# A gated mix of a spectral transform and an MLP, with gradients: the MLP as five passes over all rows, in memory of its own beside the transform

## The chip, the cores and the metric

The kernel runs on one core of a Trainium2 chip. A core has TensorE (PE, matrix products into PSUM), VectorE (DVE), ScalarE (ACT), GpSimd (POOL) and SyncE (SP, here only a queue that issues DMAs), each with its own instruction queue worked off in order, and DMA engines that move data between HBM and the on-chip memory SBUF. The metric is the device time of one execution in microseconds (us); of several runs the median counts.

## The reference

Inputs are bf16. S is 2048 rows, D is 1024, F is 3584. What has to come out is the mixed output and the gradients of eight inputs (not of B_x, which is a constant that the forward pass does not use).

```python
def A(x, w_r, w_i):                       # spectral branch
    X = rfft2(x.astype(float32)) * (w_r + 1j * w_i)
    return irfft2(X, s=(S, D)).astype(bfloat16)
def B(x, w1, b1, w2, b2):                 # MLP branch
    h = x @ w1 + b1
    r = where(h > 0, h, 0)
    return (r * r) @ w2 + b2
g   = sigmoid((A_x * gate_w).sum(-1, keepdims=True))
out = g * A(A_x, A_w_r, A_w_i) + (1 - g) * B(A_x, B_w1, B_b1, B_w2, B_b2)
# returned: out, then d(out . grad_out) by A_x, w_r, w_i, w1, b1, w2, b2, gate_w
```

The MLP is six products of the same size: h (x by w1), dh (the gradient by w2 turned, times 2 r), out (h squared by w2), dx (dh by w1 turned), dW2 (h squared turned by the gradient) and dW1 (x turned by dh). Each is 896 matmuls of 128x512.

## The kernel before

The program is written with a tile framework. The kernel names tiles in pools, the framework orders the instructions of each engine before the run, puts in the waits, and pulls an instruction forward when its inputs and tiles are free by the framework's own reckoning; on the chip each engine then follows that order. A pool that is opened where another was closed gets its memory only when the closed pool is done.

All of the work stands in one function. Rows are taken as 16 tiles of 128 (row p*16+t is partition p of tile t). DMAs go alternately through SP and POOL by `dma` (L170, the issuing line of most DMAs is L171); some name SP themselves. Its stages:

- **Rows** (L289 to L304): for each of 16 tiles the input row x and the gradient row go through `load_row` (L280: load, eight turns of 128x128 on PE, a copy by ACT into xT or goT) and `s1` (L247: adds on VectorE, eight matmuls into pk, a copy ft by ACT, eight column matmuls into pu, L266, a copy u, a store to z_scr). The gate of each row is computed here (sgate, gcol; omg is one minus the gate).
- **Middle** (L382 to L418): eight pairs of frequencies; `spectrum` (L313), the products with the weights w, `inverse` (L350), a store to y_scr; the gradients of w_r and w_i. The weights come by the loads of L385.
- **Transform out** (L424 to L460): 32 rows; r is read back from y_scr (L427), matmuls pki (L431) and pui (L437), ACT copies rt and e, adds, a store to a_scr or gx_scr.
- **Scaling** (L462 to L472): the turned gradient goT is multiplied by omg.
- **Row blocks** (L512 to L655): four times, for 512 rows each: 28 times a block of 128 hidden columns (ph, L550; ReLU and square by ACT, L554, L555; pd, L558; dhT by VectorE, L559; eight turns ptr, L566, to have h and dh with rows on partitions, copies into h2S and dhS, L568, L570, stores to h2_scr and dh_scr); then out (acc, L586) with w2 chunks w2c loaded anew for each block of rows and each half of the columns; then dx (accg, L643) with turned w1 chunks, made in the first row block (L618) and read back as w1Ttc in the other three.
- **Weight gradients** (L659 to L734): x and gradient rows lie in SBUF as 2 x 16 tiles, h and dh come by groups of 512 hidden columns (`load_fg`, L669), dW2 (L695) and dW1 (L703), then row sums for the gradients of b2 and gate_w as 64 matmuls (L713, L719), and that of b1.

The transform's pools (fconst, fbuf, fps2, fps1) are closed at the end of the transform; those of the MLP (p1blk, p1w, p1s, p1ps, p1acc, p1tr) are opened after that in the same memory, and those of the weight gradients after these.

Of the kernel before, what the change touches and what calls it, by code (L numbers as in the profile page):

```python
# [10 lines left out]
P = 128  # L11
# [6 lines left out]
FDT = FP16  # L18
# [112 lines left out]
def kernel(  # L131
# [30 lines left out]
    S2, DC, DW, DCH, FC = g.S2, g.DC, g.DW, g.DCH, g.FC  # L162
# [5 lines left out]
    dma_rr = _RR([nc.sync, nc.gpsimd])  # L168

    def dma(out, in_):  # L170
        return dma_rr().dma_start(out=out, in_=in_)  # L171
# [6 lines left out]
    pers = ctx.enter_context(tc.tile_pool(name="pers", bufs=1))  # L178
    dram = ctx.enter_context(tc.tile_pool(name="dram", bufs=1, space=bass.MemoryType.DRAM))

    identb = pers.tile([P, P], BF16, name="identb", tag="identb")
    dma(identb[:], cten["identb"].ap())
    pxt_ctx = ExitStack()
    pxt = pxt_ctx.enter_context(tc.tile_pool(name="pxt", bufs=1))
    xT = pxt.tile([P, DC, S], BF16, name="xT", tag="xT")
    goT = pxt.tile([P, DC, S], BF16, name="goT", tag="goT")

    gatew_bc = pers.tile([P, D], BF16, name="gatew_bc", tag="gatew_bc")
    dma(gatew_bc[:], gate_w.partition_broadcast(P))
    gcol = pers.tile([P, S2], FP32, name="gcol", tag="gcol")  # L190
    omg = pers.tile([P, S2], FP32, name="omg", tag="omg")
    gcs = pers.tile([P, S2], FP32, name="gcs", tag="gcs")
    gpg = pers.tile([P, S2], FP32, name="gpg", tag="gpg")
    aGo = pers.tile([P, S2], FP32, name="aGo", tag="aGo")
    bGo = pers.tile([P, S2, DCH], FP32, name="bGo", tag="bGo")
    dsc = pers.tile([P, S2], FP32, name="dsc", tag="dsc")
    dsc_bf = pers.tile([P, S2], BF16, name="dsc_bf", tag="dsc_bf")
    gb1part = pers.tile([P, FC, g.NSB], FP32, name="gb1part", tag="gb1part")
    b1col = pers.tile([P, FC], FP32, name="b1col", tag="b1col")
    ones_bf = pers.tile([P, P], BF16, name="ones_bf", tag="ones_bf")  # L200
    nc.vector.memset(ones_bf[:], 1.0)
    b2row = pers.tile([1, D], BF16, name="b2row", tag="b2row")
    dma(b2row[:], B_b2.rearrange("(o d) -> o d", o=1))

    with tc.tile_pool(name="b1tmp", bufs=1) as tp_, tc.tile_pool(name="b1ps", bufs=1, space=bass.MemoryType.PSUM) as pp_:
        b1row = tp_.tile([FC, P], BF16, name="b1row")
        dma(b1row[:], B_b1.rearrange("(fc p) -> fc p", p=P))
        b1ps = pp_.tile([P, FC], BF16, name="b1ps")
        nc.tensor.transpose(b1ps[:], b1row[:], identb[:FC, :FC])
        nc.vector.tensor_copy(out=b1col[:], in_=b1ps[:])  # L210

    a_scr = dram.tile([S2, P, D], FDT, name="a_scr")
    gx_scr = dram.tile([S2, P, D], FDT, name="gx_scr")
    z_scr = [dram.tile([S2, P, D], FDT, name=f"z_scr{T}") for T in range(2)]
    y_scr = [dram.tile([S2, P, D], FDT, name=f"y_scr{T}") for T in range(2)]
    SC = S // P
    w2T_scr = dram.tile([FC, P, DC, P], BF16, name="w2T_scr")
    w1T_scr = dram.tile([DCH, FC, P, DW], BF16, name="w1T_scr")
    h2_scr = dram.tile([g.FG, SC, P, g.FGW], BF16, name="h2_scr")
    dh_scr = dram.tile([g.FG, SC, P, g.FGW], BF16, name="dh_scr")  # L220

    YS = inv_sd / XS
    sgate = pers.tile([P, S2], FP32, name="sgate", tag="sgate")
    Q = D // 4
    H = 2 * Q
    LW = g.Df + 1
    with ExitStack() as fx:
        fc_ = fx.enter_context(tc.tile_pool(name="fconst", bufs=1))
        fb = fx.enter_context(tc.tile_pool(name="fbuf", bufs=1))
        ps2 = fx.enter_context(tc.tile_pool(name="fps2", bufs=3, space=bass.MemoryType.PSUM))  # L230
        ps1 = fx.enter_context(tc.tile_pool(name="fps1", bufs=2, space=bass.MemoryType.PSUM))

        def const(name, dt=FDT):
            arr = consts[name]
            t_ = fc_.tile(list(arr.shape), dt, name="k_" + name, tag=name)
            nc.sync.dma_start(out=t_[:], in_=cten[name].ap())
            return t_

        kf = const("kf")
        cf = const("cf")  # L240
        amat = const("amat")
        sgn = const("sgn", FP32)
        ki = const("ki")
        ci = const("ci")
        apmat = const("apmat")

        def s1(T, i, xt, kmat):  # L247
            uv = fb.tile([P, 2, H], FDT, name="uv", tag="uv", bufs=2)
            nc.vector.tensor_tensor(out=uv[:, 0, :], in0=xt[:, 0:H], in1=xt[:, H:D], op=ALU.add)
            nc.vector.tensor_tensor(out=uv[:, 1, :], in0=xt[:, 0:H], in1=xt[:, H:D], op=ALU.subtract)  # L250
            f = fb.tile([P, 4, Q], FDT, name="f", tag="f", bufs=2)
            a0, a1 = uv[:, :, 1:Q], uv[:, :, H - 1 : Q : -1]
            nc.vector.tensor_tensor(out=f[:, 0:2, 1:Q], in0=a0, in1=a1, op=ALU.add)
            nc.vector.tensor_tensor(out=f[:, 2:4, 1:Q], in0=a0, in1=a1, op=ALU.subtract)
            nc.gpsimd.tensor_copy(out=f[:, 0::3, 0:1], in_=uv[:, :, 0:1])
            nc.gpsimd.tensor_copy(out=f[:, 2:0:-1, 0:1], in_=uv[:, :, Q : Q + 1])
            pk = ps2.tile([P, 8, P], FP32, name="pk", tag="ps2")
            fl = f[:].rearrange("p a b -> p (a b)")
            for b in range(8):
                nc.tensor.matmul(pk[:, b, :], lhsT=fl[:, b * P : (b + 1) * P], rhs=kmat, start=True, stop=True)  # L260
            ft = fb.tile([P, 8, P], FDT, name="ft", tag="ft", bufs=2)
            nc.scalar.copy(out=ft[:], in_=pk[:])  # L262
            pu = ps2.tile([P, 2, H], FP32, name="pu", tag="ps2")
            o = 0
            for (b, bank, lo, n, st) in FWD:
                nc.tensor.matmul(  # L266
                    pu[:, bank, lo : lo + n], lhsT=ft[:, b, :], rhs=cf[:, o : o + n],
                    start=bool(st & 1), stop=bool(st & 2), skip_group_check=True,
                )
                o += n  # L270
            u = fb.tile([P, H, 2], FDT, name="u", tag="u", bufs=3)
            nc.any.tensor_copy(out=u[:].rearrange("p j b -> p b j"), in_=pu[:])
            dma(z_scr[T][:].rearrange("c (p i) l -> i (c p) l", i=S2)[i], u[:].rearrange("p j b -> p (j b)"))


        FWD = (
            (4, 0, 0, H, 1), (0, 0, 0, Q + 1, 0), (1, 0, 0, Q + 1, 0), (5, 0, Q + 1, Q - 1, 2),
            (6, 1, 0, Q, 1), (7, 1, 0, Q, 2), (2, 1, Q, Q, 1), (3, 1, Q, Q, 2),
        )
        def load_row(i, T):  # L280
            xt = fb.tile([P, D], BF16, name=f"nat{T}", tag=f"nat{T}", bufs=2)
            dma(xt[:], (go_perm if T else x_perm)[i])
# [23 lines left out]
        def pair(m):  # L306
            return (m, S2 - m) if m else (0, S2 // 2)
# [457 lines left out]
```

## Time and profile before

| what | us |
|---|---|
| runs | 2092.59, 2093.56, 2100.51; median 2093.56 |
| the profiled execution | 2091.43 |
| its span, first to last instruction | 2089.6 |
| PE busy in it | 1642.3 (79%) |
| VectorE busy | 566.9 (27%) |
| ScalarE busy | 564.1 (27%) |
| POOL busy | 447.5 (21%) |

The page of the profile gives these sums, a line of tenths per engine over 40 slices, the DMA queues and the costliest groups of instructions. Other views of the trace used below: busy time by stretches of time, groups by source line, the instructions of one tile, and instructions in order of time. A row of a group has, behind the bar, the busy time and the mean length of one instruction, and behind the second bar how long the engine was idle just before such instructions, with what ended that idle time. Matmuls are pipelined, so the length of one is more than its share of PE's time. A line with "x8" in the timeline is eight instructions merged.

### The profile page before, as it was taken

How to read it: one execution, taken by the hardware profiler on the slowest of the kernel's cores; microseconds unless marked ns; L12 is line 12 of the kernel's file. 1: busy time of each engine (PE TensorE's matmuls, PEld its weight loads, DVE VectorE, ACT ScalarE, POOL GpSimd, SP SyncE). 2: the span in 40 equal slices, each digit the busy share in tenths (PEclk: the TensorE clock that was granted, in tenths of full speed). 3: DMA queues.
4: the chain of work that ended last, by engine and by line, in shares of the span. 5: the costliest groups of instructions: out<-in, count | busy, mean ns of one | idle time of the engine just before them, and what ended most of it. 6: DMA issues, size and time to landing. Idle time of an engine off the chain costs nothing. (4 is left out here: it accounts for less than half of the span.)

```text
span 2089.6 us, 23144 instructions
## 1 busy us (share of the span) xinstructions
PE 1642.3 (79%) x8586; PEld 772.8 (37%) x8586; DVE 566.9 (27%) x1272; ACT 564.1 (27%) x786; POOL 447.5 (21%) x784
## 2 busy tenths in 40 slices
PE   5555555454588887899878998779978789999998
PEld 4442222232244433444323443234423234444443
DVE  4447997432522112222122221122211100000000
ACT  5662323333344312244001430004430011111111
POOL 2220101000422125322122221222131332221200
PEclk8887775555799999999999999999988989999999
DMA  6334433322366556655444554345483463333310
GB/s 211 117 101 146 160 117 118 124 97 86 118 220 204 169 177 194 191 176 186 152 142 153 180 162 161 123 130 181 156 292 106 141 212 119 119 110 101 105 38 28
DMA packets 184401, 304.09 MB, mean 146 GB/s; under 512 B 24207, under 2 KB 120991, under 8 KB 184032
## 3 DMA queue, kind: packets, MB, share of 16 engines
q1 hardware_dynamic: 138480, 161.78, 23.9%
q0 software_dynamic: 45808, 140.83, 20.7%
q8 instruction: 67, 1.10, 0.2%
q14 instruction: 46, 0.38, 0.1%
HBM read 206.03 MB, written 96.49 MB: 145 GB/s over the span
## 5 line engine op out<-in xcount | busy, mean ns | idle before, releaser
L586 PE MATMUL acc<-w2c,h2T 128*128 128x512 bf16 x896 | 216.0, 397 | 47.2 <-DMA w2c<-in_B_w_dram 38.3
L550 PE MATMUL ph<-xT,w1g 128*128 128x512 bf16 x896 | 235.8, 386 | 0.4 <-ACT rT L554 0.4
L643 PE MATMUL accg<-w1Ttc,dhT 128*128 128x512 bf16 x672 | 171.9, 393 | 57.0 <-DMA w1Ttc<-w1T_scr 48.6
L695 PE MATMUL pw<-go,h2l 128*128 128x512 bf16 x896 | 201.5, 387 | 10.6 <-ACT wo L697 4.3
L703 PE MATMUL pw<-dhl,x 128*128 128x512 bf16 x896 | 194.5, 379 | 0.0
L558 PE MATMUL pd<-goT,w2Tfc 128*128 128x512 bf16 x672 | 160.2, 379 | 0.0
L643 PEld LDWEIGHTS <-dhT 128*128 128x128 bf16 x896 | 87.5, 100 | 180.6 <-issue 105.5
L586 PEld LDWEIGHTS <-h2T 128*128 128x128 bf16 x896 | 90.3, 101 | 168.5 <-issue 77.8
L568 ACT COPY h2S<-ptr 128x512 bf16<-128x512 bf16 x112 | 65.7, 586 | 313.4 <-PE ptr L566 217.6
L695 PEld LDWEIGHTS <-h2l 128*128 128x128 bf16 x896 | 88.6, 99 | 122.3 <-issue 13.7
L559 DVE SCALAR_TENSOR_TENSOR dhT<-pd,rT 128x512 bf16<-128x512 f32 x112 | 77.3, 691 | 201.8 <-PE pd L558 194.3
L703 PEld LDWEIGHTS <-x 128*128 128x128 bf16 x896 | 87.5, 98 | 105.9
L715 DVE CAST r<-pb 1x512 bf16<-1x512 f32 x2 | 1.4, 680 | 400.7 <-PE pb L713 400.7
L554 ACT ACTIVATE rT<-ph,b1col 128x512 bf16<-128x512 f32 x112 | 77.1, 689 | 119.3 <-PE ph L550 117.8
L550 PEld LDWEIGHTS <-w1g 128*128 128x128 bf16 x896 | 79.9, 99 | 58.6 <-issue 5.6
L697 ACT CAST wo<-pw 128x512 bf16<-128x512 f32 x56 | 32.9, 587 | 253.1 <-PE pw L695 240.6
L266 PE MATMUL pu<-k_cf,ft 128*128 128x256 f16 (+3 forms) x256 | 48.8, 347 | 59.9 <-ACT ft L262 59.9
L555 ACT ACTIVATE h2T<-rT 128x512 bf16<-128x512 bf16 x112 | 70.4, 629 | 90.2 <-PE acc L586 80.3
L558 PEld LDWEIGHTS <-w2Tfc 128*128 128x128 bf16 x672 | 65.5, 98 | 78.9 <-issue 1.0
L437 PE MATMUL pui<-k_ci,rt 128*128 128x256 f16 (+3 forms) x256 | 63.7, 425 | 37.5 <-ACT rt L433 37.5
L597 DVE SCALAR_TENSOR_TENSOR ot<-a_pc,gcs,bsc 128x512 bf16<-128x512 f16 x32 | 23.8, 750 | 242.6 <-ACT bsc L595 236.5
L171 POOL DMA_DIRECT2D out_dram<-wo x56 | 30.4, 542 | 276.1 <-ACT wo L705 140.8
(209 smaller groups left out, 2109.1 us busy)
## 6 DMA issues: line engine op xcount, KB each, us to landing
w1g<-in_B_w_dram SPq DMA_DIRECT2D x14, 1024.0 KB, 5.4
w1g<-in_B_w_dram POOLq DMA_DIRECT2D x14, 1024.0 KB, 6.3
w2c<-in_B_w_dram SPq DMA_DIRECT2D x28, 512.0 KB, 3.5
w2c<-in_B_w_dram POOLq DMA_DIRECT2D x28, 512.0 KB, 4.0
w2Tfc<-w2T_scr SPq DMA_DIRECT2D x42, 256.0 KB, 3.9
w2Tfc<-w2T_scr POOLq DMA_DIRECT2D x42, 256.0 KB, 3.5
w1Ttc<-w1T_scr SPq DMA_DIRECT2D x84, 128.0 KB, 2.1
w1Ttc<-w1T_scr POOLq DMA_DIRECT2D x84, 128.0 KB, 2.3
```

The lines of the kernel that those rows point to most:

```text
L266: nc.tensor.matmul(pu[:, bank, lo : lo + n], lhsT=ft[:, b, :], rhs=cf[:, o : o + n], start=bool(st & 1), stop=bool(st & 2), skip_group_che ...
L437: nc.tensor.matmul(pu[:, bank, lo : lo + n], lhsT=rt[:, b, :], rhs=ci[:, o : o + n], start=bool(st & 1), stop=bool(st & 2), skip_group_che ...
L550: nc.tensor.matmul(ph[:], lhsT=w1g[:, dc, fcg * P : (fcg + 1) * P], rhs=xT[:, dc, cols], start=(dc == 0), stop=(dc == DC - 1))
L554: nc.scalar.activation(rT[:], ph[:], ACT.Relu, bias=b1col[:, fc : fc + 1])
L555: nc.scalar.activation(h2T[:, fc, :], rT[:], ACT.Square)
L558: nc.tensor.matmul(pd[:], lhsT=w2Tf[:, ec, :], rhs=dbT[:, ec, cols], start=(ec == 0), stop=(ec == DC - 1))
L559: nc.vector.scalar_tensor_tensor(out=dhT[:, fc, :], in0=pd[:], scalar=2.0, in1=rT[:], op0=ALU.mult, op1=ALU.mult, accum_out=gb1part[:, fc, ...
L568: nc.scalar.copy(out=stg[:, :, fcg * P : (fcg + 1) * P], in_=ptr[:])
L586: nc.tensor.matmul(accs[i][:], lhsT=h2T[:, fc, i * P : (i + 1) * P], rhs=w2c[:, r_, :], start=(fc == 0), stop=False)
L643: nc.tensor.matmul(accs[i][:], lhsT=dhT[:, fc, i * P : (i + 1) * P], rhs=w1Tt[:], start=(fc == 0), stop=(fc == FC - 1))
L695: nc.tensor.matmul(pw[:], lhsT=h2l[sc][:, fb * P : (fb + 1) * P], rhs=db_t[sc][:, ecols], start=(sc == 0), stop=(sc == SC - 1))
L703: nc.tensor.matmul(pw[:], lhsT=x_t2[sc][:, db * P : (db + 1) * P], rhs=dhl[sc][:], start=(sc == 0), stop=(sc == SC - 1))
```

## The change

The function is rewritten below the constants. The transform's arithmetic stays, and so does that of the MLP; order, memory and transfers change.

- Loads go through SP (`ld`), stores through POOL (`st`).
- Pools have a side: the transform's SBUF pools (f1, f2, f3) and two PSUM pools (fps, four banks; tps, two banks, for turns of both parts) on the right, the MLP's on the left. Their sizes are such that f2 (the largest of the transform) and the pools of the first MLP pass lie in SBUF together. A pool that takes the place of a closed one waits tile by tile (`reuse_waits="tile"`), not for the whole pool.
- `load_rows` also scales the gradient row by omg and turns the scaled row into dbT, so the stage that scaled goT goes. The transform's matrices for the middle come by pair (two loads for each m), not whole.
- Pass 1 and 2 (`mlp_in`): h and dh for one block of 128 hidden columns over all 2048 rows, xT and dbT resident; w1 and w2 are turned once here; h and dh are stored in both forms.
- Pass 3 and 4 (`mlp_grads`): dW2 with the scaled gradient rows resident, then dW1 with the x rows resident, each over seven groups of 512 hidden columns.
- Pass 5 (`mlp_out`), in two halves: out with all of w2 resident, dx with all of turned w1 resident, by blocks of 256 rows of the turned h and dh.
- The bias b2 is added by VectorE and not by a matmul; the row sums are kept by VectorE and end in two f32 matmuls each.

The new parts in the order in which the program runs them, cut:

```diff
+    ld, st = nc.sync.dma_start, nc.gpsimd.dma_start
+    def pool(name, side="left", space=SBUF, stack=None, bufs=1):
...
+        kw = {} if space == DRAM else dict(side=side, reuse_waits="tile")
...
+    fps, fps_s = pool("fps", "right", PSUM)
+    tps, tps_s = pool("tps", "right", PSUM)
...
+    def load_rows():
+        fb, fbs = pool("f1", "right")
...
+        for i in range(NT):
...
+            turned(xT, xt, i, nc.scalar.copy)
...
+            nc.vector.tensor_scalar(out=db[:], in0=go[:], scalar1=omg[:, c_], scalar2=None, op0=ALU.mult)
+            turned(dbT, db, i, nc.vector.tensor_copy)
...
+            one_s1(fb, cf, 0, i, xt, kf[:])
+            one_s1(fb, cf, 1, i, go, kg[:])
...
+    def mlp_in():
+        wb, wbs = pool("m1")
+        mps, mpss = pool("mps1", "left", PSUM)
...
+        for fp in range(FC // 2):
+            w1g = wb.tile([P, DC, PW], BF16, name="w1g", tag="w1g", bufs=2)
+            ld(out=w1g[:], in_=w1v[:, :, fp * PW : (fp + 1) * PW])
+            h2S = wb.tile([P, NT, PW], BF16, name="h2S", tag="stg", bufs=3)
+            dhS = wb.tile([P, NT, PW], BF16, name="dhS", tag="stg", bufs=3)
+            for f2 in range(2):
...
+                h2T = wb.tile([P, S], BF16, name="h2T", tag="h2T", bufs=2)
+                dhT = wb.tile([P, S], BF16, name="dhT", tag="dhT", bufs=2)
+                for sb in range(S // SW):
...
+                        mm(ph[:], lhsT=w1g[:, dc, fs], rhs=xT[:, dc, ss], start=(dc == 0), stop=(dc == DC - 1))
...
+                        mm(pd[:], lhsT=w2T[:, ec, :], rhs=dbT[:, ec, ss], start=(ec == 0), stop=(ec == DC - 1))
...
+                        st(out=w1T_scr[fc], in_=w1T[:].rearrange("p c d -> p (c d)"))
+                    if sb % 2 == 1:
...
+                            eng = nc.scalar.copy if (k_ == 0 and sb == 1) else nc.vector.tensor_copy
+                            eng(out=stg[:, b0 : b0 + 8, fs], in_=ptr[:])
...
+                st(out=h2T_scr[fc], in_=h2T[:])
+                st(out=dhT_scr[fc], in_=dhT[:])
+            fg, pr = divmod(fp, NPR)
+            st(out=h2_scr[fg][:, :, pr * PW : (pr + 1) * PW], in_=h2S[:])
+            st(out=dh_scr[fg][:, :, pr * PW : (pr + 1) * PW], in_=dhS[:])
...
+    def mlp_grads():
+        wb, wbs = pool("m2")
...
+        def group(scr, fg):
+            t_ = wb.tile([P, NT, FGW], BF16, name="grp", tag="grp", bufs=2)
+            ld(out=t_[:], in_=scr[fg][:])
...
+            ld(out=db[:], in_=go_perm[t])
...
+            nc.vector.tensor_scalar(out=db[:], in0=db[:], scalar1=omg[:, t : t + 1], scalar2=None, op0=ALU.mult)
...
+                V(out=acc[:], in0=acc[:], in1=db[:], op=ALU.add)
...
+    BW = 2 * P
+    def blocks(wb, scr):
+        v_ = scr[:].rearrange("c p s -> p c s")
+        def one(k):
+            t_ = wb.tile([P, FC, BW], BF16, name="hblk", tag="hblk", bufs=2)
+            ld(out=t_[:], in_=v_[:, :, k * BW : (k + 1) * BW])
...
+    def mlp_out():
+        wp, wps = pool("w2p")
+        w2 = wp.tile([P, FC, D], BF16, name="w2", tag="w2")
+        w1T = wp.tile([P, FC, D], BF16, name="w1Tr", tag="w1Tr")
...
+        for fc in range(0, FC, 4):
+            ld(out=w2[:, fc : fc + 4, :], in_=B_w2[fc * P : (fc + 4) * P, :].rearrange("(q p) e -> p q e", p=P))
...
+                    acc = mps.tile([P, H], FP32, name="acc", tag="acc", bufs=4)
+                    for fc in range(FC):
+                        mm(acc[:], lhsT=cur[:, fc, t2 * P : (t2 + 1) * P], rhs=w2[:, fc, cs], start=(fc == 0), stop=(fc == FC - 1))
...
+    run(chain(load_rows(), fft_mid(), fft_out()))
+    run(mlp_in())
+    run(mlp_grads())
+    tps_s.close()
+    fps_s.close()
+    run(mlp_out())
```

`run` only exhausts a generator, so the program names the transform's instructions first, then those of each pass.

More of the change, by code (lines that the diff above doesn't have):

```diff
@@ L188 @@
-    gatew_bc = pers.tile([P, D], BF16, name="gatew_bc", tag="gatew_bc")
[L189 to L210, printed above, removed]
@@ L435 @@
[L435 to L442 removed]
+                pu = fps.tile([P, 2, H], FP32, name="pui", tag="ps2", bufs=2)
+                column_stage(INV, pu, rt, ci)
@@ L738, with chain, run @@
+    def chain(*gens):
+        for g_ in gens:
+            yield from g_
+    def run(gen):
+        for _ in gen:
+            pass
+    run(chain(load_rows(), fft_mid(), fft_out()))
[4 more added lines that the diff above has]
+    run(mlp_out())
 _INS = ['A_x', 'A_w_r', 'A_w_i', 'B_x', 'B_w1', 'B_b1', 'B_w2', 'B_b2', 'gate_w', 'grad_out']
```

833 lines of the change are left out of this document (384 added, 449 removed).

## The prediction

> **What bounds the kernel now.** First the busy time by stretch, cut where the stages change: rows (stage 1 of the transform), middle, transform out, scaling of the turned gradient, four row blocks of the MLP, weight gradients, tail. The columns are busy us of each engine with instructions, granted clock, DMA share, GB/s.
>
> ```profile
> core 0: us, PE busy (x) PEld busy (x) DVE busy (x) ACT busy (x) POOL busy (x), PEclk, DMA share, GB/s
> 0.00:171.00 171.00, 96.21 (x793) 72.65 (x793) 73.81 (x185) 104.88 (x116) 37.20 (x104) 0.82 0.43 148
> 171.00:345.00 174.00, 100.58 (x473) 38.02 (x474) 160.98 (x257) 48.90 (x42) 17.06 (x24) 0.69 0.40 129
> 345.00:541.00 196.00, 91.53 (x491) 54.84 (x489) 70.77 (x195) 61.68 (x64) 11.38 (x21) 0.53 0.32 102
> 541.00:560.00 19.00, 11.76 (x52) 5.63 (x52) 16.96 (x17) 5.42 (x17) 15.47 (x5) 0.60 0.35 117
> 560.00:1668.00 1108.00, 934.22 (x4923) 420.15 (x4921) 239.52 (x615) 277.43 (x436) 276.03 (x462) 0.96 0.53 171
> 1668.00:2070.00 402.00, 394.46 (x1795) 176.39 (x1796) 2.04 (x5) 65.28 (x112) 88.82 (x167) 0.98 0.34 111
> 2070.00:2089.60 19.60, 13.54 (x64) 5.16 (x62) 2.84 (x5) 0.46 (x1) 1.56 (x3) 0.98 0.02 7
> ```
>
> The reader is to see three states. The transform takes 541 us with PE busy 288 at a clock of 0.82 to 0.53; VectorE is full only in the middle (161 of 174). The row blocks are PE's, yet not at its rate. The weight gradients are nearly that rate, which the chain of waits in order of time gives, with the first and last of the pieces that repeat:
>
> ```profile
> 1710.65 27.63 PE pw L703 x128
> ...
> 1904.03 27.63 PE pw L695 x128
> ```
>
> 128 matmuls of 128x512 in 27.63 us are 0.216 us each. The MLP has six products of 896, so 5376 x 0.216 = 1161 us that both kernels need. The four row blocks hold 3584 of them (774 us) and 1344 turns of 128x128; 1108 - 774 - 75 leaves 259 us. The groups by line say what PE waited for:
>
> ```profile
> L586 PE MATMUL acc<-w2c,h2T 128*128 128x512 bf16 x896 | 216.0, 397 | 47.2 <-DMA w2c<-in_B_w_dram 38.3 <-DVE gx L648 4.2 <-DVE bGo L602 4.0
> L643 PE MATMUL accg<-w1Ttc,dhT 128*128 128x512 bf16 x672 | 171.9, 393 | 57.0 <-DMA w1Ttc<-w1T_scr 48.6 <-DVE bGo L602 6.4 <-DVE gx L648 0.9
> L523 PE MATMUL ptw<-identb,w2r 128*128 128x128 bf16 x224 | 18.3, 228 | 25.5 <-ACT h2S L568 20.3 <-DMA w2r<-in_B_w_dram 5.2
> L431 PE MATMUL pki<-k_ki,r 128*128 128x128 f16 x256 | 33.2, 311 | 68.7 <-DMA r<-y_scr 68.6
> L266 PE MATMUL pu<-k_cf,ft 128*128 128x256 f16 (+3 forms) x256 | 48.8, 347 | 59.9 <-ACT ft L262 59.9
> ```
>
> Single durations here are pipelined and no rate; the idle column counts. Weight chunks that arrive just in time (38.3, 48.6), staging copies held by a store (20.3); in the transform, y rows (68.6) and ACT's evictions (59.9). The rest of the 259 lies between matmuls. The waits are latencies with no other work placed behind them.
>
> Is other work put there when there is some? The tile views of w and w2c, and PE's timeline in the first row block:
>
> ```profile
> L385 SPq DMA_DIRECT2D w<-in_A_w_r_dram x8: 373/375/657, 20.7 to 289.0; - x8
> L171 SPq DMA_DIRECT2D w2c<-in_B_w_dram x28: 367/381/529, 568.6 to 1575.0; - x28
> 616.74 0.61 PE L523 MATMUL ptw<-identb,w2r 128*128 128x128 bf16 x8
> 617.19 1.24 PE L550 MATMUL ph<-xT,w1g 128*128 128x512 bf16 x5
> 618.27 1.89 PE L558 MATMUL pd<-goT,w2Tf 128*128 128x512 bf16 x8
> 620.00 0.39 PE L566 MATMUL ptr<-identb,h2T 128*128 128x128 bf16 x4
> 620.22 0.81 PE L550 MATMUL ph<-xT,w1g 128*128 128x512 bf16 x3
> 621.03 0.40 PE L566 MATMUL ptr<-identb,dhT 128*128 128x128 bf16 x4
> 621.26 0.61 PE L523 MATMUL ptw<-identb,w2r 128*128 128x128 bf16 x8
> ```
>
> The transform's w loads stand behind the whole row loop in the program, yet the first goes at 20.7, about 150 us ahead; w2c goes at 568.6, while the blocks of h and dh still have to run (the cycle shown is at 617). And three ph of the next block stand before the last turns (ptr of dhT) of the present one. So the order on an engine is not that of the program: work whose tiles are free is pulled forward. In the kernel before, the MLP's pools take the transform's place, so nothing of it could be.
>
> **The change part by part.** *PE's own work.* One block of 128 hidden columns in this cycle takes 621.26 - 616.74 = 4.52 us for 16 matmuls and 16 turns; 8 turns are 617.19 - 616.74 = 0.45, one 0.056. At the rate it would be 16 x 0.216 + 16 x 0.056 = 4.35, so a factor of 1.04. The first pass does per block of 128, over all 2048 rows, 64 matmuls and 48 turns: 13.8 + 2.7 = 16.5, with the factor 17.2; 28 blocks 481 us. The transform at full rate: rows 32 x (16 turns 0.90 + 2305 columns 0.97) = 60; middle 32 x 8 x 0.216 = 55 and some 216 small ones at a turn's price, 12, together 67; out 32 x (0.45 + 0.97) = 45. Sum 172.
>
> *VectorE and ScalarE in the first pass.* Prices:
>
> ```profile
> L559 DVE SCALAR_TENSOR_TENSOR dhT<-pd,rT 128x512 bf16<-128x512 f32 x112 | 77.3, 691 | 201.8 <-PE pd L558 194.3 <-issue 3.8 <-ACT rT L554 3.2
> L559 DVE DVE_READ_ACCUMULATOR dhT<-pd,rT 128x1 f32 x112 | 9.3, 83 | 0.0
> L346 DVE CAST x<-px 128x1024 f16<-128x1024 f32 x16 | 19.5, 1220 | 20.5 <-PE px L345 20.5
> L300 DVE TENSOR_SCALAR kg<-k_kf,gcol 128x128 f16<-128x128 f16 x16 | 4.0, 252 | 5.7 <-ACT gcol L297 5.7
> L570 DVE COPY dhS<-ptr 128x512 bf16<-128x512 bf16 x112 | 47.6, 425 | 138.5 <-DMA dh_scr<-dhS 74.7 <-PE ptr L566 53.8 <-PE pd L558 10.0
> L445 DVE TENSOR_TENSOR tt<-e 128x512 f16<-128x512 f16 x32 | 13.6, 426 | 115.7 <-ACT e L443 115.7
> L371 DVE TENSOR_TENSOR pc<-v 128x1024 f16<-128x1024 f16 x14 | 9.7, 690 | 1.8 <-ACT v L367 1.6
> L286 ACT COPY goT<-pt 128x1024 bf16<-128x1024 bf16 x16 | 16.3, 1018 | 0.0
> L554 ACT ACTIVATE rT<-ph,b1col 128x512 bf16<-128x512 f32 x112 | 77.1, 689 | 119.3 <-PE ph L550 117.8 <-issue 1.4
> L555 ACT ACTIVATE h2T<-rT 128x512 bf16<-128x512 bf16 x112 | 70.4, 629 | 90.2 <-PE acc L586 80.3 <-POOL goT L472 6.6
> ```
>
> A turned 128x1024 piece in bf16 on VectorE isn't in the trace; it lies between 0.43 (one of 512) and 0.85 (two). I take 0.69, as the two add rows go from 426 at 512 to 690 at 1024. Per block VectorE then has 4 x (0.69 + 0.08 to read the accumulator) + 5 x 0.69 = 6.5 us, 183 in all; ScalarE 4 x (0.69 + 0.63) + 1.02 = 6.3. Both are under PE's 17.2.
>
> *Stage A, transform with the first pass beside it.* They lie in separate SBUF and PSUM, so I expect the pulling forward seen above, transform first.
> Rows: bound by a chain of PE, ACT, PE, ACT per half row; ACT loses the goT copy (16 x 1.02), VectorE gains scale and turn. 171 before; I take 155 (145 to 171). Only two blocks can be open (h2T and dhT have two buffers), so PE does at most 1.8 blocks here.
> Middle: VectorE's 161 of transform work stay and come first. What the MLP gets of it lies between nothing (stage 174, no block) and 70 us (stage 238, 10.7 blocks, PE then full). I take 35, near the low end because the stage is 92% full already: 5.4 blocks in (161 + 35)/0.97 = 202.
> Rest: PE has 45 + (28 - 1.8 - 5.4) x 17.2 = 403, VectorE about half of it, so PE sets it: 403.
> Staging: h2S and dhS share three buffers, so each pair of blocks waits for the store of the pair before. Same bytes as before, where PE lost 20.3 to them and VectorE 74.7; I take 14, between 0 and 75.
> Queues: all loads now stand on SP, some 150 in A at 0.3 to 0.5 us of issue each, and a w1g that waits for its buffer holds the transform's next z or r behind it. Between nothing and the 68.6 that y rows cost PE before; I take nothing, since PE has blocks to do meanwhile. On POOL the small f copies of the row loop stand behind stores that wait for evictions; only two blocks store there, nothing.
> A = 155 + 202 + 403 + 14 = 774. With nothing in the middle the rest is 45 + 26.2 x 17.2 = 496 and A = 155 + 174 + 496 + 14 = 839; with all of it 155 + 238 + 311 + 14 = 718.
> The terms 172 and 45 want a full clock. The transform ran at 0.53 in its last stage (row 345 to 541). At 0.53 the 45 are 85, A is 40 longer. I take the full clock, as in the rows from 560 on, because PE will not pause there. [...]
>
> *DMA in A.* The queues' rows give the rate:
>
> ```profile
> q1 hardware_dynamic: 138480, 161.78, 23.9%
> q0 software_dynamic: 45808, 140.83, 20.7%
> w1g<-in_B_w_dram SPq DMA_DIRECT2D x14, 1024.0 KB, 5.4
> ```
>
> 161.78 MB in 23.9% of 16 x 2089.6 engine-us are 20.2 GB/s an engine, 324 for 16; the software queue the same with packets nearly three times as long, so pieces of 512 bytes should cost by their bytes. A pair of blocks moves 4.72 MB out (h2T, dhT, w1T, h2S, dhS) and 1.05 in: 17.8 us of 34.4. With the transform's rows beside it DMA is at some 60%.
>
> *Stage B, both weight gradients.* 1792 x 0.216 = 387. Its tiles lie where xT lay, so 16 gradient rows and the first group (6.3 MB, 19 us at 324) start after the last ph and pd, and VectorE scales and sums each row, about 1.7 us (the sum priced as the 128x1024 f32 cast, 1.22; the scale between 0.25, the row of kg, and 0.69, I take 0.5), 27 in all. Between 15 (what the kernel before loses there, 402 - 387) and 40; I take 28. The column sums, now two f32 matmuls, 3. B = 418. The 64 row-sum matmuls of the tail go.
>
> *Stages C and D, out and dx.* 387. The 224 small DMAs of w2c and w1Ttc and their 87 us of PE waits go, as w2 and turned w1 are resident. Hidden-block loads are 1.84 MB for 24 us of matmuls, 6 at the rate. What comes instead: w2 lies over the group buffers of B, so its 7.3 MB start after B's last matmul, 23 us at 324 and a first landing of 5.4. Four accumulators hold 24 us of matmuls that can follow the chunks; so the stall is 5 if they do, 28 if one accumulator stands in line alone. I take 15. Turned w1 follows behind and is due 190 us later. VectorE has per row tile some 3 x 1.22 + 4 x 0.69 = 6.4 us beside PE's 12.1. 5 for small gaps. C + D = 407.
>
> *Tail:* last add, store, two column sums: 10, of 19.6 before.
>
> **Sum:** 774 + 418 + 407 + 10 = 1609 of span, against 2089.6. The profiled execution's time is 2091.43 and the median 2093.56, so 4 us more: **1613**.
>
> **The rivals.** *No overlap.* The MLP's instructions stand behind the transform's in the program; if the ordering looks only a short way ahead, the stages follow each other: 155 + 174 + 196 + 481 + 14 = 1020 for A, in all 1859. For it: the program runs the transform's parts to their end first. Against: w, 150 us early.
>
> *The waits come back.* The order is fixed before the run; if DMAs and evictions land later than it assumed, PE waits in line though other work is ready. The row blocks lost 259 us over 3584 matmuls, 72 ns each. Put on the first pass (28 x 64) and on C and D (1792), without B, that lost none, 129 + 129 less the 34 I have for it: 1837. For it: both kernels fix the order the same way. Against: the largest named waits were for weights, and those are resident now.
>
> *Slower than before: the stores of the first pass.* All stores go through POOL's queue. If 5.77 MB a pair land slower than 34.4 us, the staging and h2T buffers hold VectorE, then PSUM, then PE, pair by pair. It passes 2090 when a pair takes 68.7 us (481 more over 14), that is below 84 GB/s. Against: 171 GB/s in the row of the four blocks, 102 in the idlest stage, and POOL's issue costs the same beside a busy VectorE and an idle one:
>
> ```profile
> L171 POOL DMA_DIRECT2D z_scr<-u x32 | 17.3, 540 | 101.1 <-ACT u L272 98.2 <-PE pk L260 2.9
> L171 POOL DMA_DIRECT2D out_dram<-wo x56 | 30.4, 542 | 276.1 <-ACT wo L705 140.8 <-ACT wo L697 134.8 <-issue 0.4
> ```
>
> [...]
>
> **How the numbers follow.** Forecast 74% (3 of it below 1500, from the full middle with the least of every other term: 718 - 24 + 405 + 392 + 8 = 1499). The waits come back 12%, no overlap 9%, the stores 4%, others 1%. The low end is that 1500; the high end must take in the second rival whole, since the forecast's own upper end, 839 for A, 12 and 13 more for the two starts, the slow clock's 40 and staging at its 75, is 1800: 1500 to 1840. Outside remain the 3, most of no overlap and the stores. Within 0.5%, about what a measurement of this kernel can tell from no change: 1%. Slower: 4%. Faster: 95%.
>
> **What would show it.** ph and pd from 30 us on among pk and pu; first pass ending near 774, PE clock 0.9 and more after the rows. PE idle some 28 us between the last pd and a steady pw, some 15 between the last pw and a steady acc, none named w2 or w1T later. PE's busy share 90% and more from 360 us on. Wrong would be: ph only after the last pui (no overlap); PE idle behind stg copies or POOL (stores); a first pass in which PE is idle in many pieces of 1 to 5 us released by DMAs or VectorE (the waits come back); VectorE above 95% after the middle, my 0.69 being too low.

## The result, and the profile after

The changed kernel takes **1670.84 us** (median of four runs, 1669.16 to 1674.24) beside 2097.03 (2092.59 to 2105.31) for the kernel before: ratio 0.797, 95% interval 0.794 to 0.800. The forecast was 1613, range 1500 to 1840. The profiled execution took 1669.16 us with a span of 1667.4; numbers below are from it. Each time below is the median of four runs, and only the run with both edits has one far off the others, 2862.23 us at a granted clock of 0.80 beside 1616.60 to 1619.30, which its ratio leaves out. From here on line numbers are those of the changed kernel unless said otherwise.

Busy time by stretch, columns as in the prediction, cut where the stages end: rows; middle; transform out; rest of the first pass; start of the weight gradients; weight gradients; out and dx; tail.

```profile
0.00:142.00 142.00, 81.45 (x815) 59.90 (x815) 92.45 (x237) 92.50 (x103) 42.11 (x100) 0.98 0.54 170
142.00:318.00 176.00, 96.14 (x453) 35.03 (x452) 157.02 (x248) 43.41 (x38) 21.10 (x30) 0.67 0.48 132
318.00:432.00 114.00, 110.83 (x893) 68.56 (x892) 67.76 (x201) 82.16 (x95) 26.06 (x46) 0.98 0.69 225
432.00:842.00 410.00, 409.94 (x2729) 216.06 (x2727) 146.75 (x323) 153.63 (x221) 67.50 (x99) 1.00 0.53 170
842.00:850.00 8.00, 0.62 (x5) 0.32 (x5) 3.85 (x9) 0.00 (x0) 3.86 (x4) 0.69 0.94 333
850.00:1261.50 411.50, 399.06 (x1796) 176.60 (x1796) 28.44 (x36) 64.95 (x111) 45.35 (x84) 0.96 0.39 140
1261.50:1656.40 394.90, 388.76 (x1793) 175.74 (x1792) 172.52 (x283) 0.59 (x1) 18.13 (x32) 0.99 0.53 163
1656.40:1667.40 11.00, 2.01 (x5) 0.25 (x4) 2.05 (x3) 0.00 (x0) 1.05 (x2) 0.70 0.06 24
```

From 318 to 1656 PE is busy nearly without a pause, at a mean granted clock of 0.96 to 1.00 but for 0.69 in the 8 us from 842. Before that, for 318 us, it is idle 44% of the time: only 178 of it busy, with VectorE at 157 of 176 in the middle, as before.

Where the first pass begins is told by the tile views: name, count, shortest, median and longest duration in ns, then the first and the last start.

```profile
L321 PE MATMUL si<-y,apmat x32: 166/212/212, 140.7 to 311.9; 128*128 128x2 f16 x32
L484 PE MATMUL ptw<-identb,w2r x224: 216/219/314, 312.8 to 826.4; 128*128 128x128 bf16 x112
L499 PE MATMUL pd<-dbT,w2T x896: 379/379/634, 317.8 to 840.9; 128*128 128x512 bf16 x180
L255 PE MATMUL pui<-ci,rt x256: 272/273/390, 330.1 to 430.9; 128*128 128x256 f16 x64, 128*128 128x512 f16 x32, 128*128 128x257 f16 x32
L486 DVE COPY w2T<-ptw x28: 684/692/693, 317.1 to 826.6; 128x1024 bf16<-128x1024 bf16 x28
```

The first turn of w2 (ptw, L484) starts at 312.8, beside the last `si` (L321) of the middle at 311.9, and the first pd at 317.8. The transform's last stage (pui) does have the first pass beside it; rows and middle have none of pd.

PE's largest waits, in us in total, times, longest (some of the small ones of rows and middle left out):

```profile
PE pv L319 <- DVE y L366: 53.2, 16, 5.2
PE pu L255 <- ACT ft L235: 37.0, 30, 1.9
PE px L292 <- DVE pm L281: 22.5, 8, 3.0
PE pw L591 <- DVE res L567: 10.8, 15, 1.6
PE b1ps L430 <- DMA b1row<-in_B_b_dram: 7.9, 1, 7.9
PE acc L665 <- DMA w<-in_B_w_dram: 6.1, 1, 6.1
PE pw L591 <- DMA grp<-h_scr: 5.7, 1, 5.7
```

The weight chunks, staging copies and y rows that stood in this list before (38, 49, 20, 69 us) are gone. What is left above 20 us is in rows and middle: y and pm from VectorE, ft from ScalarE.

### The profile page after: what moved, and what is told of

The parts are those of the page before. It is cut to its first block, busy times and chain, and to the rows that moved or that the text cites. A ratio compares the mean times of both kernels' runs of the same rounds, so it can differ in the third digit from the quotient of the medians.

```text
span 1667.4 us, 20915 instructions
## 1 busy us (share of the span) xinstructions
PE 1488.8 (89%) x8482; PEld 732.5 (44%) x8482; DVE 670.8 (40%) x1334; ACT 437.2 (26%) x566; POOL 225.2 (14%) x395
## 4 chain that ended last, share of the span: by engine, by line
issue 68%; POOL 9%; PE 0%; ACT 0%; POOLq 0%; DVE 0%
POOL out_dram L609 2%; POOL dh_scr L524 1%; POOL out_dram L598 1%; POOL w1T_scr L510 1%; POOL h2T_scr L520 1%; POOL dhT_scr L521 1%; POOL ax_scr L414 1%; POOL out_dram L706 1%; POOL h_scr L523 1%; POOL out_dram L672 1%; PE pui L255 0%; ACT rt L401 0%; ACT e L405 0%; POOL out_dram L534 0%; POOLq L609 0%
## 5 line engine op out<-in xcount | busy, mean ns | idle before, releaser
L591 PE MATMUL pw<-res,grp 128*128 128x512 bf16 x896 | 203.9, 388 | 18.0 <-DVE res L567 10.8
L499 PE MATMUL pd<-dbT,w2T 128*128 128x512 bf16 x896 | 215.3, 381 | 3.1 <-DVE w2T L486 3.1
L665 PE MATMUL acc<-w,hblk 128*128 128x512 bf16 x896 | 195.6, 382 | 6.1 <-DMA w<-in_B_w_dram 6.1
L603 PE MATMUL pw<-grp,res 128*128 128x512 bf16 x896 | 193.5, 379 | 0.0
L703 PE MATMUL accg<-w1Tr,hblk 128*128 128x512 bf16 x896 | 193.5, 379 | 0.0
L591 PEld LDWEIGHTS <-grp 128*128 128x128 bf16 x896 | 88.7, 99 | 133.3 <-issue 26.4
L665 PEld LDWEIGHTS <-hblk 128*128 128x128 bf16 x896 | 88.1, 98 | 113.6 <-DMA w<-in_B_w_dram 6.6
L499 PEld LDWEIGHTS <-w2T 128*128 128x128 bf16 x896 | 87.4, 98 | 106.5 <-DVE w2T L486 8.1
L703 PEld LDWEIGHTS <-hblk 128*128 128x128 bf16 x896 | 87.7, 98 | 105.7
L603 PEld LDWEIGHTS <-res 128*128 128x128 bf16 x896 | 87.7, 98 | 105.7
L255 PE MATMUL pu<-cf,ft 128*128 128x256 f16 (+3 forms) x256 | 38.7, 293 | 38.1 <-ACT ft L235 37.0
## 6 DMA issues: line engine op xcount, KB each, us to landing
dh_scr<-dhS POOLq DMA_DIRECT2D x14, 1024.0 KB, 10.6
```

Source lines behind the costliest of these rows:

```text
L255: mm(pu[:, bank, lo : lo + n], lhsT=ft[:, b, :], rhs=mat[:, o : o + n], start=bool(f_ & 1), stop=bool(f_ & 2), skip_group_check=True,)
L499: mm(pd[:], lhsT=w2T[:, ec, :], rhs=dbT[:, ec, ss], start=(ec == 0), stop=(ec == DC - 1))
L591: mm(pw[:], lhsT=cur[:, t, fb_ * P : (fb_ + 1) * P], rhs=res[t][:, hf * H : (hf + 1) * H], start=(t == 0), stop=(t == NT - 1),)
L603: mm(pw[:], lhsT=xr[t][:, d_ * P : (d_ + 1) * P], rhs=cur[:, t, :], start=(t == 0), stop=(t == NT - 1),)
L665: mm(acc[:], lhsT=cur[:, fc, t2 * P : (t2 + 1) * P], rhs=w2[:, fc, cs], start=(fc == 0), stop=(fc == FC - 1))
L703: mm(acc[:], lhsT=cur[:, fc, t2 * P : (t2 + 1) * P], rhs=w1T[:, fc, cs], start=(fc == 0), stop=(fc == FC - 1))
```

## The experiments

The theory for the 58 us that the time is above the forecast: the first pass starts late because its turns (ptw, ptq, ptr) share the two buffers `tr` with the transform's (pt, sp, si), and buffers of one tag are handed out in the order in which the program names them, so ptw has to stand behind the last si. The rival: VectorE, full in the middle, has no room anyway.

**Own buffers for the turns.** The two banks are split, one for the transform (pt, sp, si, b1ps), one for the MLP (ptw, ptq, ptr, pb1):

```diff
-            pt = tps.tile([P, DC, P], BF16, name="pt", tag="tr", bufs=2)
+            pt = tps.tile([P, DC, P], BF16, name="pt", tag="tr", bufs=1)
...
-                ptw = tps.tile([P, DC, P], BF16, name="ptw", tag="tr", bufs=2)
+                ptw = tps.tile([P, DC, P], BF16, name="ptw", tag="trm", bufs=1)
...
```

> The one PSUM tag of two buffers for small turns is split: one buffer for the transform (pt, sp, si), one for the first MLP pass (ptw, ptq, ptr). Theory 'buffer order': a tag's buffers are handed out in program order, so in the changed kernel the first turn of w2 (312.8 us, just behind the last si) had to stand behind every transform tile of that tag; with a buffer of its own the first pd comes before 40 us, several blocks of 128 hidden columns are done by the end of the middle, and the time falls to 1590 to 1640 from 1671. Rival 'VectorE is full': in the rows and the middle the evictions of the first pass come last on a full VectorE, so it starts early and makes at most two blocks by the end of the middle, and the time stays within 1650 to 1690, single-buffered turns costing what the early start brings.

Measured 1652.46 us (1650.38 to 1653.04), ratio 0.789 (0.786 to 0.792). The tile views, and the first 136 us of the middle (its last si starts at 313.4):

```profile
L484 PE MATMUL ptw<-identb,w2r x224: 216/219/314, 17.1 to 810.6; 128*128 128x128 bf16 x112
L499 PE MATMUL pd<-dbT,w2T x867: 376/379/634, 61.0 to 825.0; 128*128 128x512 bf16 x174
```
```profile
142.00:278.00 136.00, 86.15 (x464) 34.87 (x467) 129.28 (x206) 41.55 (x40) 20.46 (x28) 0.79 0.66 191
```

ptw moves from 312.8 to 17.1, so the order of the buffers was what held it. But the gain is 18 us, and the time lies in the rival's range: the same view restricted to pd counts 46 up to 142 and 46 from there to 318, of 32 a block, so 2.9 blocks and not 7.2. VectorE is at 129 of 136. Both theories have a part, one behind the other. The edit has a price of its own, too. With one buffer for the turns instead of two, PE waits for w2T, the copy of the turned piece, 25 times:

```profile
PE pd L499 <- DVE w2T L486: 20.3, 25, 1.0
```

In the changed kernel that is one wait of 3.1 us. It is 3.2 in the next run, which keeps two shared buffers, and 20.6 in the one behind it, which does not. So the 18 us are what the early start brought less some 17, an estimate from these rows.

**Copies of the middle to ScalarE.** The second of each pair of evictions of px and pv (L306, L326; 32 in all) goes from VectorE to ScalarE; the turns share buffers as in the changed kernel.

```diff
-            (nc.scalar.copy if j == 0 else nc.vector.tensor_copy)(out=x[:, j, :, 0:H], in_=px[:])
+            nc.scalar.copy(out=x[:, j, :, 0:H], in_=px[:])
...
```

> The 32 copies of px and pv that VectorE does in the middle (1.22 us each, 39 us of 157 busy in 176) go to ScalarE (43 busy). Nothing else changes, so the first pass still starts behind the last si. If the middle is bound by VectorE's sum, it shortens by 25 to 39 us and the time is 1632 to 1646. Rival: it is bound by the chain from product to product, then by less than 10 us, time 1661 to 1675.

Measured 1628.35 us (1624.53 to 1635.11), ratio 0.778 (0.775 to 0.781).

```profile
L321 PE MATMUL si<-y,apmat x32: 166/212/212, 139.9 to 277.7; 128*128 128x2 f16 x32
L484 PE MATMUL ptw<-identb,w2r x224: 216/219/314, 278.7 to 792.0; 128*128 128x128 bf16 x112
```

The last si is at 277.7 and not 311.9, and ptw follows it as before: VectorE sets the middle's length. The profiled execution, the slowest of the four, gained 34 us, which is what the stage gained; the median gained 42.

**Both edits.**

> Both edits. Buffer order: with VectorE relieved the first pass gets room in the middle, more than the sum of the two gains, 1550 to 1600. VectorE is full: only the second edit counts, 1630 to 1660.

Measured 1618.45 us, ratio 0.773 (0.770 to 0.776): 52 below the changed kernel, where the two alone gave 18 and 42. In the middle

```profile
142.00:278.00 136.00, 94.92 (x552) 40.88 (x556) 125.50 (x225) 77.95 (x77) 24.57 (x34) 0.85 0.64 204
```

VectorE is still at 92% and PE at 70%. The time lies between the two theories' ranges: with VectorE eased, own buffers add 10, net of the 20.6 us of waits for w2T, and VectorE is still the fuller of the two.

**No overlap.** The first pass's pool goes to the side of the transform and waits for its end as a whole, so the stages follow each other.

```diff
...
-        wb, wbs = pool("m1")
+        wb, wbs = pool("m1", "right", reuse="pool")
```

> The SBUF pool of the first pass (m1) is put into the memory of the transform's pools with a wait for the whole pool, so the pass starts when the transform ends; the five passes with their resident operands stay. Theory 'overlap counts': the changed kernel hides the transform's last stage (114 us with PE full, 45 of it transform work) beside the first pass; alone it takes 150 to 196, so 105 to 155 are added, 1775 to 1825. Rival 'residence counts': the gain is in the passes, little is added, below 1720.

Measured 1740.22 us (1734.68 to 1742.21), ratio 0.830 (0.827 to 0.834): the overlap with transform out is worth 69 us, less than expected, because the transform's last stage is itself quick now, 104 us where the kernel before took 196:

```profile
330.00:434.00 104.00, 53.95 (x504) 40.07 (x502) 49.83 (x155) 59.83 (x62) 16.53 (x31) 0.96 0.48 155
```

**Why that stage was slow before.** In addition, the rows read back (r) and the results (yo) share three buffers, as they did in the kernel before:

```diff
-                r = fb.tile([P, H, 2], FDT, name="r", tag="r", bufs=3)
+                r = fb.tile([P, H, 2], FDT, name="r", tag="u", bufs=3)
...
-                yo = fb.tile([P, D], FDT, name="yo", tag="yo", bufs=2)
+                yo = fb.tile([P, D], FDT, name="yo", tag="u", bufs=3)
```

> The version with the first pass held until the transform's end (1740 us), where the transform's last stage stands alone in about 125 us, against 196 in the kernel before; here r and yo share one tag of three buffers again, as before the change. Theory 'buffers': with three buffers for both, r can be loaded only one row ahead, PE waits for it, the stage goes back to 170 to 200, 1785 to 1815. Rival 'queues': the wait for r came from stores on SP ahead of it, all stores are on POOL now, so nothing changes, 1732 to 1750.

Measured 1837.90 us (1835.61 to 1840.88), ratio 0.877 (0.873 to 0.882), 98 above the run without overlap and more than either theory expected. The stage, PE's wait and SP's:

```profile
330.00:545.00 215.00, 101.00 (x520) 58.81 (x521) 52.18 (x161) 64.29 (x64) 17.39 (x32) 0.52 0.26 85
```
```profile
PE pki L399 <- DMA r<-y_scr: 81.3, 24, 14.9
SPq L395 <- DMA ax_scr<-yo: 183.7, 30, 12.2
```

Twice the time, near the 196 of the kernel before: the load of r waits until a result is stored. Shared buffers alone make the stage that slow, with every store on POOL. The load queue is not cleared for the kernel before. There SP waited 87.4 us for such stores before it could issue r (line numbers of the kernel before):

```profile
SPq L427 <- DMA gx_scr<-yo: 55.7, 14, 8.7
SPq L427 <- DMA a_scr<-yo: 31.7, 16, 3.3
SPq L171 <- DVE yo L451: 86.0, 23, 8.9
```

The last line is as much again: stores of yo on the same queue, ahead of the next load of r, that waited for VectorE. What each of the two was worth there is not shown.

**Weights streamed again.** out and dx by 512 rows, with w2 and turned w1 loaded in chunks for each block and half, all on SP; the rest as changed.

```diff
-        w2 = wp.tile([P, FC, D], BF16, name="w2", tag="w2")
-        w1T = wp.tile([P, FC, D], BF16, name="w1Tr", tag="w1Tr")
...
+            t_ = wb.tile([P, 4, H], BF16, name="w2c", tag="w2c", bufs=2)
+            ld(out=t_[:], in_=B_w2[fc * P : (fc + 4) * P, cs].rearrange("(q p) e -> p q e", p=P))
...
+            t_ = wb.tile([P, H], BF16, name="w1Tt", tag="w1Tt", bufs=3)
+            ld(out=t_[:], in_=w1T_scr[fc][:, cs])
```

> The changed kernel with out and dx undone to chunks: blocks of 512 rows, four accumulators, w2 in chunks of 512 KB with two buffers and turned w1 in chunks of 128 KB with three, each loaded anew for each block and half, as in the kernel before, but all on SP's queue. Nothing resident; first pass and weight gradients as in the changed kernel. Theory 'residence': the waits for w2c and w1Ttc come back, 87 us of PE or up to 72 ns for each of 1792 matmuls, 129 us; 1755 to 1800. Rival 'queue and order': the waits before came from loads that stood behind waiting stores on the same queue, so on SP alone the chunks come in time, 1665 to 1700.

Measured 1879.34 us (1878.81 to 1890.50), ratio 0.898 (0.893 to 0.903), 208 above.

```profile
PE acc L679 <- DMA w2c<-in_B_w_dram: 89.1, 22, 31.8
PE accg L736 <- DMA w1Tt<-w1T_scr: 73.3, 66, 14.0
```

These two waits are 162 of it, and 31.8 of them a single wait at the start of out. Of all that the runs took back one at a time this is the largest, and larger than expected. It is not what the resident operands saved against the kernel before, which lost 87 us to these waits on two queues: one queue with all the chunks was worse than that, and the two effects are not separated.

**Loads and stores alternating over SP and POOL**, as before (those that named a queue before still do):

```diff
-    ld, st = nc.sync.dma_start, nc.gpsimd.dma_start
+    turn_ = _RR([sp, pq])
+    def ld(out, in_):
+        return turn_()(out=out, in_=in_)
+    st = ld
```

> The changed kernel with its DMAs handed to SP and POOL in turn, loads and stores mixed, as before the change (the loads of constants, w, z and r stay on SP, those of the gradients of w on POOL). Theory 'queues': a load behind a store that waits for its data comes late, the rows stage goes from 142 towards 171 and loads of the passes hold PE, 1710 to 1790. Rival: the order on a queue is made so that it doesn't matter, 1660 to 1690.

Measured 1697.42 us (1692.15 to 1700.37), ratio 0.810 (0.806 to 0.815), between the two ranges: the split is worth 27 us, most of it at the two starts, while the first ptw, behind the middle's last si, moves only from 312.8 to 314.0 (lines are six further down here):

```profile
PE pw L597 <- DVE res L573: 24.5, 7, 16.4
PE acc L671 <- DMA w<-in_B_w_dram: 17.4, 5, 6.1
```

None of the runs took back the first pass over all rows by itself, the stage that scaled goT, or the row sums of the tail, so their shares of the 426 us between the two kernels are not measured.

**The two starts.** Three attempts at taking the loads ahead of the stage that needs them. First the pool of the weight gradients on the other side, with its second half's row tiles asked for first, w2's place free for loading early, and turned w1 on the other side as well:

```diff
-        wb, wbs = pool("m2")
+        wb, wbs = pool("m2", "right")
+        xr = [wb.tile([P, D], BF16, name=f"res1_{t}", tag=f"res1_{t}") for t in range(NT)]
```

> Memory of the later passes laid out so that their first loads need not wait: the weight gradients' pool (m2) goes to the side that the transform has left, with the tiles that are loaded late at its near end; turned w1 goes over m2, w2 and the hidden blocks over xT's and the first pass's memory. If the idle PE at the two starts (26 and 6 us) is the wait for that memory, it goes but for 0 to 6 us: 1638 to 1650. If it is the transfer or the scaling of the rows itself, it stays, 1660 or more.

Measured 1678.92 us (1669.22 to 1681.37), ratio 0.800 (0.796 to 0.805): the start of out was gone, that of the weight gradients not (24.5 us of PE's waits for the group and 6.5 for row tiles), and the time no shorter. I put it down to w2's 7.3 MB, which stood ahead on SP. The next two take w2 behind those loads and ask for the first operand group and the first row tiles first, once on the changed kernel and once on top of both edits above. W2 is loaded in the third group, and a one-column copy by ScalarE into each piece stands ahead of its load:

```diff
+        first = wb.tile([P, NT, FGW], BF16, name="grp", tag="grp0")
...
+            if n == 2:
+                wp, wps = pool("w2p")
```

> The changed kernel with only the two starts changed. Of the weight-gradient pass, the first operand group and the row tiles that it starts with are allocated first on the far side, where the transform ended, so that they need none of the first pass's memory; W2 for the out pass is loaded in the third of its 14 groups, behind the weight-gradient pass's own loads on SP. (In the earlier attempt the row tiles of the second half had that place, and W2's 7.3 MB stood ahead.) If the start of the weight-gradient pass waits for memory and for the order on SP's queue, both starts go: 18 us of TensorE waits and the 8 us before the first matmul at the one, 6 at the other, so 1638 to 1650 us, with the first product of that pass within 3 us of the first pass's last matmul. If it waits for something else, such as the stores of h and their return, only the 6 us go and it is 1662 to 1670, with the first product 15 us or more behind.

Measured 1668.04 us (1660.20 to 1670.35), ratio 0.795 (0.792 to 0.798).

> The two starts together with the first pass's own buffers for turned tiles and the 32 copies moved to ScalarE (1618 us for these two without the starts). Its first and third stretch wait at other places than the starts, so if the three are independent it gives 1618 less 20 to 32, so 1586 to 1598 us. If the row tiles' loads and scalings, 16 of each on VectorE, now in the first pass, are in that pass's way, or what the transform left to do is merely moved, 1605 to 1625 us.

Measured 1616.28 us (1612.81 to 1617.62), ratio 0.771 (0.769 to 0.774). Both on the side of nothing gained at that start: my reading fell. In the first of the two, SP's wait and PE's:

```profile
SPq L566 <- DMA h2T_scr<-h2T: 50.7, 1, 50.7
PE pw L601 <- DMA grp<-h_scr: 13.4, 1, 13.4
PE pw L601 <- DVE res L569: 8.4, 13, 2.0
```

The first row tile's load waits 50.7 us for a store of h2T, a tile of the first pass. So its memory was still that pass's, although the pool lay on the other side and asked for this tile among its first. The last attempt changes only this: what is needed first gets a pool of its own, opened first.

```diff
-        wb, wbs = pool("m2", "right")
-        first = wb.tile([P, NT, FGW], BF16, name="grp", tag="grp0")
+        wa, was = pool("m2a", "right")
+        first = wa.tile([P, NT, FGW], BF16, name="grp", tag="grp0")
+        row0 = [wa.tile([P, D], BF16, name=f"res0_{t}", tag=f"res0_{t}") for t in range(NT)]
+        acc = wa.tile([P, D], FP32, name="dbacc", tag="dbacc")
+        wb, wbs = pool("m2", "right")
```

> As the run of all three, with one thing changed: the first operand group, the 16 row tiles and their sum now form a pool of their own on the far side, opened before the pool of the rest. In the run before, all of them were one pool, and the first load of a row tile was issued only 53 us after everything but a store of h from the first pass's tile had ended, so the tiles that the pool asked for first did not lie where the transform had been. If it is the place in memory that holds the start of the weight-gradient pass, the loads now go out in the middle of the first pass, the 25 us of waits at the start (13.5 for the first group, 8.5 for the row tiles, 2 around) go down to under 4, and the time is 1588 to 1598 us. If it is the order on SP's queue or VectorE's scaling of the row tiles (1.53 us each, 24 in all) that sets the start, the waits merely move into the first pass or stay, and the time is 1608 to 1620 us.

Measured **1589.23 us** (1585.60 to 1591.03), ratio 0.760 (0.757 to 0.764), the fastest of all. Its tile views and a piece of PE's timeline (start, length, what):

```profile
L569 SPq DMA_DIRECT2D res<-in_grad_out_dram x16: 328/432/1680, 390.3 to 422.5; - x16
L603 PE MATMUL pw<-res,grp x896: 379/379/389, 795.0 to 991.4; 128*128 128x512 bf16 x180
```
```profile
794.58 0.61 PE L516 MATMUL ptr<-identb,h2T 128*128 128x128 bf16 x8
795.03 0.81 PE L603 MATMUL pw<-res,grp 128*128 128x512 bf16 x3
796.21 0.61 PE L516 MATMUL ptr<-identb,dhT 128*128 128x128 bf16 x8 [0.37 <-DVE h2S L518]
```

The loads go out at 390 to 422, and pw of the weight gradients stands among the last turns of the first pass, with no wait but the 0.37 us shown. It is 1618 less 29, near the 24 to 26 of that start and the 6 of the next. Between this run and the one before, only the pools differ, so place in memory is what held the start; whether it would have gone with W2 ahead on SP is not shown.

## Why the prediction was right, and where it was off

The mechanism was right in the later stages: operands that stay in SBUF keep PE busy, and the first pass fills the transform's last stage. It was wrong for the first 312 us, where nothing overlaps, and the sum is 58 us short: 1609 of span forecast, 1667.4 measured. By its terms:

- **Stage A** ends at 842, forecast 774: here lie 68, more than the whole error. Rows 142 instead of 155, middle 176 instead of 202, staging nothing instead of 14; the rest 842 - 318 = 524 instead of 403. The step that failed is "work whose tiles are free is pulled forward", with its 1.8 blocks in the rows and 5.4 in the middle: 7.2 x 17.2 = 124 us of PE work put where none was done. I had asked whether SBUF and PSUM were separate, not whether a tag was shared: `tps` holds turns of both parts. And 35 us of VectorE's time in the middle were an estimate too high by itself, as the run with own buffers shows (1.4 blocks there, 5.4 forecast). The step cost some 95 us, 121 in the rest less the 26 by which a middle without blocks is shorter. That the sum is only 58 short is in part luck: rows and staging came out 27 below the forecast and the later stages 10, which hid 37 of the 95.
- **A bound that could not be.** The low end lets the middle take 10.7 blocks in 238 us, but by the prediction's own prices PE would need 67 + 10.7 x 17.2 = 251 for that.
- **The price of a block** held. 28 x 17.2 + 45 = 527 for the rest with no block done ahead; measured 524. The copy of a turned 128x1024 piece, taken as 0.69 between 0.43 and 0.85, is 692 ns.
- **The full clock** in transform out held: 0.98 beside the first pass, 0.53 before. The run without overlap shows that my reason (PE does not pause there) asks for more than was needed, as the clock was 0.96 there too with PE busy only 54 of 104 us (more on this in the last section).
- **Queues at nothing** held as far as PE's list shows, which has no wait for r or w1g above 1 us; stores of 1 MB land in 8.0 and 10.6 us, far below the 34 of a pair of blocks, so the rival of the stores was not near.

```profile
h_scr<-h2S POOLq DMA_DIRECT2D x14, 1024.0 KB, 8.0
dh_scr<-dhS POOLq DMA_DIRECT2D x14, 1024.0 KB, 10.6
```

- **Stage B** 842 to 1261.5, 419.5 for a forecast of 418: 8 before the first pw, 5.7 of them for the group's load, then 10.8 for row tiles that VectorE scales and sums, for the 28. dW2 takes 218 us here and 196 in the last run, where loads and scaling both lie in the first pass:

```profile
L591 PE MATMUL pw<-res,grp x896: 376/379/634, 850.1 to 1067.8; 128*128 128x512 bf16 x180
```

- **C and D** 394.9 for 407: the start cost 6.1 (5 to 28, 15 taken) and the gaps nothing. Tail 11 for 10.
- **The waits come back** (12%) did not happen: from 318 to 1656 PE was idle 29 us in all, the differences of the five stretches (3, 0, 7, 12 and 6). **No overlap** (9%) was half true: none for 312 us, then full. Its price was wrong too, 1859 where the run without overlap gives 1740; 92 of the 119 between are transform out at 104 instead of 196. The change gives r and yo buffers of their own there; I had read that stage's 68.6 of waits as the latency of y rows and had not looked at the tags.

## What to carry to other kernels

Two parts overlap only as far as they share no tile tag: buffers of one tag come in program order (ptw's first start was 312.8 us with the shared tag, 17.1 with its own), so the first start of each tile, beside the last start of the other part's tile of that tag, shows what ties them. Then look at which engine is full in the stretch that is to be filled; moving its work was worth more (42 us) than opening the door as it was done here (18, after some 17 lost to single buffers). Where a stage's first loads should go ahead, give their tiles a pool of their own in memory that comes free early (1616 to 1589 us here), and check what the first load waits for, not where the program names it.

## What the runs showed of the hardware

The same stage, transform out alone, took 104 us at a granted clock of 0.96 and 215 at 0.52 (PE busy 54 and 101), and the two kernels differ only in which of its tiles share buffers. In the quick one PE's waits were many and short (for rt, 32 with a longest of 1.7 us), in the slow one 24 waits for r were 3.4 us each in the mean, 14.9 the longest.

```profile
PE pui L255 <- ACT rt L401: 50.9, 32, 1.7
```

In the trace of the changed kernel the granted clock is 1.00 or 0.50 and changes 32 times between 12 and 1647 us. The shortest time between two changes is 3.41 us, and every other is a whole multiple of it. Cut into pieces of this length, laid from the rise at 223.84 us in both directions, all 479 pieces have a clock of either 1.00 or 0.50; with the cuts shifted by a quarter, a half or three quarters of a piece, 32 are mixed. Five of the pieces, columns as before:

```profile
220.43:223.84 3.41, 3.41 (x16) 1.33 (x15) 3.41 (x6) 1.49 (x2) 0.00 (x0) 0.50 0.65 245
223.84:227.25 3.41, 1.73 (x23) 0.76 (x19) 3.32 (x8) 2.34 (x2) 0.94 (x2) 1.00 0.67 193
227.25:230.67 3.42, 1.90 (x8) 0.70 (x8) 3.42 (x6) 1.01 (x1) 1.19 (x2) 1.00 1.10 245
230.67:234.08 3.41, 1.44 (x9) 0.68 (x10) 3.41 (x7) 0.00 (x0) 0.00 (x0) 1.00 0.92 235
234.08:237.49 3.41, 1.29 (x7) 0.23 (x4) 2.91 (x5) 1.01 (x1) 0.00 (x0) 0.50 0.24 57
```

The clock fell after 16 pieces with PE busy for 0.04 to 1.68 us, and rose after 16 with 2.84 to 3.41. It stayed at 1.00 after 413 with 1.54 and more, and at 0.50 after 33 with up to 2.58. In the piece before the fall at 234.08 us PE was busy for 1.44 us, and the one wait that reaches into it was 2.21 us long.

So PE did not have to be idle for a whole piece: before each of the 16 falls it was busy for less than half of one. The two stages above fit this, by an estimate from their rows: in the mean PE was busy for 1.77 us of each 3.41 in the quick one (54 of 104), above the 1.68, and for 1.60 in the slow one (101 of 215), below the 2.84. By what rule the clock is granted is not shown. The buffers that made PE wait cost 81.3 us of waits for r, and PE's busy time went from 54 us at a clock of 0.96 to 101 at 0.52.
